# A convolution and an expert layer on one core: a shift tile of half the width, layer norm by sums on ScalarE, eleven gather slots, the last output chunk accumulated in memory, first loads in other queues, and a new written order

## The chip, the cores and the metric

The kernel runs on one core of a Trainium2 chip. The metric is the device time of one execution in microseconds (us); lower is better. Engines are named as the profile names them: PE multiplies matrices, DVE is the vector engine, ACT the scalar engine with its function tables, POOL the general engine, which here mostly issues indirect transfers, and SP issues the plain transfers. SBUF is the memory on the chip in 128 partitions, PSUM the small memory that PE writes.

## The reference

Two layers share one normalised input, and their sum is returned (L = 2048 tokens, D = 448 columns; cut to what matters):

```python
xn = _layernorm(x)                         # mean and variance over the 448 columns
# layer A: a long convolution along the tokens, one filter for each column
dt = exp(log_dt)
P  = exp((dt * A)[:, :, None] * l)         # A complex, 448 x 256; l = 0..2047
K  = einsum("dn,dnl,dn->dl", C, P, dt * B).real
yA = irfft(rfft(xn, 4096) * rfft(K, 4096))[:2048] + xn * Dskip
# layer B: one expert out of 4096 for each token and each of 16 heads
q      = einsum("nd,dhc->nhc", xn, w_q)    # two halves of 256 for each head
s1, s2 = q1 @ k1.T, q2 @ k2.T              # 64 scores each
e      = argmax(s1) * 64 + argmax(s2)
act    = gelu(einsum("nd,nhd->nh", xn, u[e]))
yB     = einsum("nh,nhd->nd", act, v[e])
return x + yA + yB
```

Only the best of each half is kept, so the softmax over the chosen experts is over one element and is 1.

## The kernel before

`Kernel.plan` registers steps, each with an engine, the steps it depends on and the buffers it takes from rings and gives back. Each step belongs to a named stream. The string `ORDER`, some 3,000 characters long, is the order in which the steps are written into the program: each character names a stream through `CODE`, and takes that stream's next step. Each engine runs its own instructions strictly in the order written. A step waits where a dependency is not met or a buffer is not free, and what stands behind it on the same engine or in the same queue waits too.

The work falls into these parts:

- **Parameters.** Six parameter arrays of 448 KB and `log_dt` are loaded on SP. DVE, ACT and POOL make from them phases and decays (the tiles `pv`, `pw`, `px`), which go to the memory tensors `tp_d` and `tt_d`. `dt` goes through memory once (`dt_d`) to spread it over the partitions; `pv<-pv,dt` on POOL (L432) needs it.
- **Combine** (`combine`, 16 heads). The query weights are multiplied with the keys in advance: 32 loads `wq` of 448 KB on SP, PE's `wc` (L862), a copy on ACT, a transpose on PE, and the result kept as `W`.
- **Layer norm** (`ln`, two of the 16 tiles of 128 tokens at a time). Tile `xx` is loaded, DVE takes the statistics (`BATCH_NORM_STATS2` L909 and `BATCH_NORM_AGGREGATE` L913) and a reciprocal square root by three iterations on 128x2 numbers, ACT writes the normalised tile (L925), SP stores it as `xn_d`.
- **Input of the convolution** (`u_step`): PE `up` (L724), ACT `vst` (L727), a store to `vu_d`.
- **Scores** (`score`): PE `sc` (L961, L970), the maximum and its index on DVE and ACT, the index list through memory (`idx_d`) to `ig`.
- **Filter tables** (`batch`, 56 of 8 columns). PE makes exponents `lg` (L579, L581), ACT the magnitudes `mg` (L590, L592). DVE makes integer phases `ph`: a first row (L610), then four doublings that add a shifted step from the tile `st` to the rows there are (L614). `st` is made by `steps` (L547) for four batches at a time; `ph` holds two batches. ACT reads `ph` and makes cosine and sine in `CS` (L629, L632, L635). DVE's products L660, L662, L664 and L666 make `zi` and `mg` out of `mg` and `CS`, and PE sums them to `kp` (L682); `kt`, `vp` and `VK` follow.
- **Convolution** (`conv`, chunks of 128, 128, 128 and 64 columns): PE `U` from `VU` and `VK` (L798, L779 for the last chunk), ACT `us`, DVE's product `cp` (L808, L786), PE's inverse transform `ip` (L830, L825), ACT `tq` (L837), a store to `t_d` (L842).
- **Experts** (`experts`, 16 tiles, four groups of four indirect gathers): POOL gathers a row of u and v for each token and head as `ue` (L1083, 448 KB each), DVE takes the dot with the token `xr` (L1091), short steps on ACT and DVE make the factors `A` (L1114), PE sums `po` (L1121), ACT copies to `ob`, POOL issues a store that adds to the output in memory (L1136).
- **Final** (`final`, for each chunk, four groups of four token tiles): `tl` is loaded from `t_d` and `hl` from a constant, PE `po` (L1178), ACT copies, POOL issues a store that adds to the output (L1192). The last chunk is done in another way: its part of the output is loaded back as `bb`, DVE adds to it (L1182) and SP writes it with a plain store; its constant comes as one tile `hb`.

Gather slots, `wq`, `xx`, `W`, `tl`, `bb`, `hb` and others come from one pool of 4 KB tiles; the number of gather slots in it is `UE`.

Of the kernel before, what the change touches and what calls it, by code (L numbers as in the profile page):

```python
# [8 lines left out]
F32 = mybir.dt.float32  # L9
# [106 lines left out]
class Plan:  # L116
# [57 lines left out]
    "44H444HH1HH2704HH7HH2HHH46HH7HH24444I6H4444H47H8CH22NI2H4241DE4HHC88142OC78D4D127H4H1EKECH74C44FLKF4CHHDL47HDEEFKDFFL24H"  # L174
    "27EC4J42HMF2HDC227KLI272223QEI47DC44E4346CDFFDK441C4QE4C9FDE978L88FDRQ9M4CREE94J74497J75RCKF5F8LQ4KCD977R71D4wE77E9778CL"
    "FFDEDAE6YFF7AYK9QHHLQANH7OQRHR9GR8S8AH9wQZH9HRaTwRHAQGHeRQYTHRQTHGQTRTRYHNHRHOSTQJTAQGMTHTeTHbQTRTTReTQUcQdQRVeNfRIVOWgg"
    "PXRQRfQPPPxBRRggHSxQTfgRxTyHeTRggIRZxTgwMXJxQKTyxHLyyfgQKLgzxQRh!!HRNRyyOz#xSPyyHQgzT!MH#QQxxggzgJTT$h!RyhTxRxR#HQRgfhgT"
    "#HQyTbghyh$yzQx!fHz!#NxyReOyiQ#TeHTHx$gyxRwYHeyxRTwxzQeUKHSeVQR!whgLhHwRjgHgcQQKQx!PRydzgY#yHRLHTbyIJRINHR#ThgThHx$bhHhH"
    "TOgKcLkRHVaTyMSdxgzxgT!!QiHxQzRyKHxQj#eHTyPTQRTyTHhxQfyTz!Hk#H%LggRRz$JhQMxH!iHjRRfhHRgxKg#TLHkyIfYhygTW#exyeTSexiX$KLYg"
    "lxKlLNMeyjzO!IHQzHgxKy!mygLPK#yTkTMxmQ#Hyl$ggwJQRHhzLRh!Thgmg!HezQfxhRex#gK#eQHwRwxThheHyxLgRgHR$y%QfggRHNxxOUiyjwfyzQ!z"  # L180
    "TMx!hy#byZSQggVVT#cQeHxyHRykHlgHHgzx$a!hRxJHgQ!gQHzTIYmhKTy&x#gLTh#digXIKTeQRyRTLJYP$fNjggTRhRlxOgeHyyHkHQzfKgh!gLxmzHHh"
# [12 lines left out]
    "gqg$xzjy!eq#yhykorgoxspcoixgh#hypqyygwxnwb$zdoggpsqf!yhwhqayp!ehjgqegrgfohgzpehss#opxqxxogk#wpfgqoexegzhg$pyotg!!qiZhqxh"
    "xgjxiojggxppzrlhh#yk#geysqytm$lnszykm!gzixf%qre!yhgjtehgf#yhs#yxgxgx&kyhfzsggxyleeggy!gzgh!i#jtyxh#zg!h!hal$mlgxzemk(g$f"
    "geyymgfyxxheyghzg#f!z!#ehegxliw#bwgxgggjhhhkwgwg$gh#)i$ymh*yehcjgdlklyehxmf&xxggf(yyeyxhmgxzy!y%igxzjz+fg!x)(e!(gZek#gz#"
    "ygglhxhh$xy!y##yxmgx*)ghywihc$gdjzgk*ha)f*ieexbg!gjywzfggfge!xheey##ghyhggh+xilzggkgxxlg!hjhh+gmzmwe!ykX$fxyxglih#eymgf#"
    "wgx+gjh$yefxhxzxye!gzxg!yZhg#ey%#ygzxkigca!l!hyxj$gdmgghhyzgxkhlh#ey#xfyehgzg!y!yxmxxfgzgifye#yx$xjz#heg!g!egzwwgkhylxhh"
    "i$gmyjgxwfxklwyyg#h#mzogh!yn!hoxigz$pxg#oeyyxgef#e%jyqxeppqzg!$qhgofgnZoo!pqhxehrgigypzgyqkggp#xy#qhhygop$sogpgsqx&xxofo"
    "qnpaqyzgpg-erfhesooyen!qjzggh!yxtpxfs#pgegq&oxw#egypgnqhwhiu$vojzghhq&!wptrnkkhgxhgqgsie!ufzyggoeh#ghefp#es$ggjvfygxhxny"  # L200
    "%gkuolhgmileqxhpwlgjyxzhtmxiqhg!!gjmggzrxglshshklkhuh#hlmmmhhyytij&x#kxixxyyjvz!$xv(kxllmymo!oqqqryysqszox(rs#y#yy)o$ysz"
    "y!zz!#!tz!*#q,q()#q#rtss($qr*+)ts$+s*t..+).//%&::-./:/*;;:+;;")


class Kernel:
    OPT = dict(UE=8, XX=4, CS=2, ZI=2, MG=4, KT=4, HL=2, SG=1, XR=4, OB=3, XT=1, ST=1)
# [21 lines left out]
    def alloc(s):  # L228
# [11 lines left out]
        s.t_d = dr.tile([64, 2, 32, D], F32, name="t_d")  # L240
# [14 lines left out]
        s.amt = c.tile([128, 2, 4], I32, name="amt")  # L255
        s.ph = c.tile([128, 16, 2, 2, M, 2], I32, name="ph")
# [18 lines left out]
    def consts(s):  # L275
# [6 lines left out]
        def sets():  # L282
            s.nc.gpsimd.memset(s.halfpi, HALF_PI)
            s.nc.gpsimd.memset(s.one, 1.0)
            s.nc.gpsimd.memset(s.dsk, 0.0)
            for h in range(2):
                for k in range(4):
                    s.nc.gpsimd.memset(s.amt[:, h, k:k + 1], k + 2 + 6 * h)
# [98 lines left out]
    def params(s, part):  # L387
# [145 lines left out]
    def steps(s, u):  # L533
# [9 lines left out]
        def sh():  # L543
            o["st"] = s.sm.tile([128, 4, 4, 2, M, 2], I32, name="st", bufs=s.o["ST"])
            for h in range(2):
                a = s.amt[:, h]
                s.nc.vector.tensor_tensor(out=view(o["st"], 2 * M * h, [[16 * M, 4], [4 * M, 4], [1, 2 * M]]),  # L547
                                          in0=view(o["tp"][:, 0, 0], 0, [[0, 4], [1, 4 * M], [0, 2]]),
                                          in1=view(a, 0, [[1, 4], [0, 8 * M]]), op=ALU.logical_shift_left)
        x = p.add("st_ld", "SP", xf(512, 256), l, deps=s.tp_done, take=("tpl",))  # L550
        o["ready"] = [p.add("st_v", "DVE", 2 * dv(512), sh, n=1, deps=[x, s.amt_done], take=("st",))]
        return o

    def batch(s, o, ro, b, VK, col):
# [48 lines left out]
        def row(k):  # L603
            def f():
                def rw(x, y):
                    return s.ph[:, x:y].rearrange("p r b h m x -> p r (b h m x)")
                b0 = b % 4
                if k < 0:
                    for h in range(2):
# [14 lines left out]
        def four(v):  # L624
            return view(v.rearrange("p r b h m x -> p (r b h m x)"), 2 * R * (b % 2), [[2, R], [4 * R, 16], [1, 2]])
# [636 lines left out]
```

## Time and profile before

| what | us |
|---|---|
| the three runs | 777.7, 782.04, 784.82 |
| median | 782.04 |
| the profiled run | 777.9 |
| its span, from first to last instruction | 776.1 |
| first instruction of PE | 16.56 |
| first product of the convolution on DVE (L808) | 399.72 |
| start of the last product of the convolution on DVE (L786) | 747.03 |

How to read it: the profiled run is 1.8 us longer than its span, and durations below are those of this one execution. Busy time is the sum of an engine's instructions; the time ahead of an instruction in which its engine did nothing is put down to what released it. A transfer appears twice: as its issue on SP or POOL, and as the time until its data have landed.

### The profile page before, as it was taken

To read this page: it belongs to the slowest core of one execution; us is meant where nothing else is said; L and a number is where in the kernel's file an instruction comes from. 1 tells how busy PE (TensorE), PEld (TensorE's weight loads), DVE (VectorE), ACT (ScalarE), POOL (GpSimd) and SP (SyncE) were. 2 spreads that over 40 slices of the span, in tenths; PEclk is the share of its full clock that TensorE was granted. 3 is DMA by queue.
4 is the path that set the end of the run, shared out by engine and by line. 5 is a ranking of instruction groups with operands and counts; after the bars stand their busy time and mean duration, and the time that the engine had idled before them with its cause. 6 is when DMAs were issued, how large, how long until landed. Compare 5 with 4: busy or idle time off the path is not lost.

```text
span 776.1 us, 19859 instructions
## 1 busy us (share of the span) xinstructions
PE 658.5 (85%) x7628; PEld 358.9 (46%) x7628; DVE 680.7 (88%) x1727; ACT 535.7 (69%) x1071; POOL 351.3 (45%) x303
## 2 busy tenths in 40 slices
PE   1999999998999998999888967788995775899982
PEld 0434343443434344434356644456763442577751
DVE  5878659998999999999999999799998999999840
ACT  1756237457677597665668899698797998789720
POOL 2011033353623435557455474555466585744620
PEclk9999999999999999999899997566996767699995
DMA  9997956767867859778999999898898997999996
GB/s 310 355 331 287 318 163 209 261 197 243 273 205 222 260 174 310 235 239 265 319 338 329 314 345 306 271 254 269 257 315 286 348 302 237 345 296 293 274 264 125
DMA packets 139975, 212.36 MB, mean 274 GB/s; under 512 B 45096, under 2 KB 121896, under 8 KB 139816
## 3 DMA queue, kind: packets, MB, share of 16 engines
q0 software_dynamic: 29120, 124.27, 50.2%
q1 hardware_dynamic: 110760, 86.81, 36.8%
q8 instruction: 60, 0.98, 0.5%
q14 instruction: 35, 0.29, 0.1%
HBM read 181.42 MB, written 33.29 MB: 277 GB/s over the span
## 4 chain that ended last, share of the span: by engine, by line
DVE 30%; PE 29%; DMA 19%; ACT 12%; issue 7%; POOL 1%; SPq 1%; DVEq 0%; ACTq 0%; POOLq 0%
PE sc L961 10%; DMA ue<-in_uv_dram,ig 7%; DVE ue L1091 7%; DVE zi L662 3%; DVE ph L614 3%; DVE mg L666 3%; DMA xr<-xn_d 3%; PE wc L862 3%; PE kp L682 2%; PE sc L970 2%; ACT CS L629 2%; PE ip L830 2%; ACT CS L632 2%; DVE cp L808 2%; PE up L724 2%
## 5 line engine op out<-in xcount | busy, mean ns | idle before, releaser
L1083 POOL DMA_INDIRECT ue<-in_uv_dram,ig x256 | 307.3, 1200 | 334.4 <-PE po L1121 87.1
L961 PE MATMUL sc<-W,xt 128*128 128x512 f32 x384 | 181.4, 612 | 4.6 <-ACT xt L946 3.8
L1091 DVE SCALAR_TENSOR_TENSOR ue<-ue,xr 128x448 f32<-128x448 f32 x256 | 155.8, 619 | 17.4 <-DMA ue<-in_uv_dram,ig 11.6
L961 PEld LDWEIGHTS sc<-W,xt 128*128 128x128 f32 x384 | 69.7, 192 | 93.8 <-issue 82.7
L1121 PE MATMUL po<-ue,A 128*32 128x448 f32 x512 | 70.1, 616 | 10.2 <-issue 3.9
L682 PE MATMUL kp<-mg 128*32 128x64 f32 x1792 | 64.1, 240 | 14.9 <-DVE mg L666 6.5
L590 ACT ACTIVATE mg<-lg 128x512 f32<-128x512 f32 x112 | 63.2, 597 | 18.7 <-PE lg L579 17.9
L629 ACT ACTIVATE CS<-ph 128x1024 f32<-128x1024 int32 x56 | 62.7, 1120 | 8.0 <-DVE ph L614 5.4
L662 DVE TENSOR_TENSOR zi<-mg,CS 128x1024 f32<-128x1024 f32 x56 | 68.2, 1218 | 0.0
L666 DVE TENSOR_TENSOR mg<-mg,CS 128x1024 f32<-128x1024 f32 x56 | 68.2, 1217 | 0.0
L614 DVE CUSTOM_DVE_ANT_0 ph<-st,ph 128x512 uint16<-128x512 uint16 (+2 forms) x84 | 65.1, 775 | 0.3
L635 ACT ACTIVATE CS<-CS,halfpi 128x1024 f32<-128x1024 f32 x56 | 64.4, 1151 | 0.5
L682 PE MATMUL kp<-zi 128*32 128x64 f32 x1792 | 63.4, 238 | 0.0
L632 ACT ACTIVATE CS<-ph 128x1024 f32<-128x1024 int32 x56 | 63.1, 1127 | 0.1
L682 PEld LDWEIGHTS kp<-mg 128*32 128x32 f32 x1792 | 46.5, 121 | 35.3 <-issue 8.6
L702 PE MATMUL vp<-f,kt 128*64 128x128 f32 x448 | 42.0, 319 | 21.9 <-DVE kt L693 9.3
L985 DVE TENSOR_REDUCE mx<-sc 128x8 f32<-128x512 f32 x64 | 43.7, 683 | 14.5 <-PE sc L970 10.8
L579 PE MATMUL lg<-lc,rt 32*128 32x512 f32 x112 | 40.4, 564 | 14.4 <-ACT mg L590 10.8
L682 PEld LDWEIGHTS kp<-zi 128*32 128x32 f32 x1792 | 48.8, 123 | 0.1
L702 PEld LDWEIGHTS vp<-f,kt 128*64 128x64 f32 x448 | 27.8, 156 | 45.3 <-DVE kt L693 9.0
L798 PE MATMUL U<-VU,g 128*64 128x128 f32 x384 | 42.2, 299 | 5.4 <-DVE cp L808 3.4
L830 PE MATMUL ip<-cp,e 64*128 64x256 f32 x384 | 45.4, 383 | 0.2 <-ACT tq L837 0.2
(246 smaller groups left out, 1221.3 us busy)
## 6 DMA issues: line engine op xcount, KB each, us to landing
wq<-in_wq_dram SPq DMA_DIRECT2D x32, 448.0 KB
xr<-xn_d SPq DMA_DIRECT2D x64, 224.0 KB
vu_d<-vst SPq DMA_DIRECT2D x64, 112.0 KB
VU<-vu_d SPq DMA_DIRECT2D x12, 512.0 KB
t_d<-tq SPq DMA_DIRECT2D x24, 256.0 KB
tl<-t_d SPq DMA_DIRECT2D x12, 512.0 KB
ue<-in_uv_dram,ig POOLq DMA_INDIRECT x256, 6.4
xx<-in_x_dram SPq DMA_DIRECT2D x16, 224.0 KB
```

The lines of the kernel that those rows point to most:

```text
L614: s.nc.vector.tensor_tensor(out=rw(n, 2 * n), in0=rw(0, n), in1=o["st"][:, k, b0:b0 + 2].rearrange("p b h m x -> p (b h m x)")[:, None].to ...
L629: s.nc.scalar.activation(CS[:, 1].rearrange("p (m r x) -> p m r x", r=16, x=2), four(s.ph), AF.Sin, scale=SC)
L632: s.nc.scalar.activation(B["CS"][:, 0].rearrange("p (m r x) -> p m r x", r=16, x=2), four(s.ph), AF.Abs)
L635: s.nc.scalar.activation(B["CS"][:, 0], B["CS"][:, 0], AF.Sin, scale=-SC, bias=s.halfpi)
L662: V.tensor_tensor(out=zi[:, 512:], in0=mg[:, 512:], in1=CS[:, 1], op=ALU.mult)
L666: V.tensor_tensor(out=mg[:, 512:], in0=mg[:, 512:], in1=CS[:, 0], op=ALU.mult)
L682: s.nc.tensor.matmul(kp[32 * c:32 * c + 32, 64 * gi:64 * gi + 64], T[ri][:, 1024 + m:1056 + m], view(T[ri], m, [[512, 2], [1, 32]]), start ...
L702: s.nc.tensor.matmul(vp[64 * ri:64 * ri + 64, 128 * gi:128 * gi + 128], B["kt"][:, 64 * gi:64 * gi + 64], s.f1[:, ri], start=True, stop=True)
L961: s.nc.tensor.matmul(B["sc", q].rearrange("p a b -> p (a b)"), B["xt"][:, i], w, start=(q % 2 == 0 and i == 0), stop=(q % 2 == 1 and i == 2))
L1083: s.nc.gpsimd.indirect_dma_start(out=ue, out_offset=None, in_=s.io["uv"], in_offset=bass.IndirectOffsetOnAxis(ap=s.IDX[t][:, c, g:g + 1].b ...
L1091: s.nc.vector.scalar_tensor_tensor(Q["ue", c][:, :D], Q["ue", c][:, :D], 1.0, B["xr", c], op0=ALU.mult, op1=ALU.mult, accum_out=Q["dot"][: ...
L1121: s.nc.tensor.matmul(B["po"][32 * c:32 * c + 32, :D], Q["A"][:, c], Q["ue", c][:, D:], start=(g == 0), stop=(g == 3))
```

## The change

1. The shift tile `st` holds [2, 8, 2M] words in place of [4, 4, 2M, 2]: two DVE shifts of 256 elements for four batches in place of two of 512. The pair of halves `x`, innermost in `ph` before, goes outward: [row, x, h, batch, m]. The first row becomes one instruction of 128 elements in place of two of 64; the doublings keep their sizes. ACT's two reads of `ph` in `trig` and `trig2` change with it: before, two neighbouring words and then a jump of 128 words, now single words with a jump of 64 words (256 bytes).
2. Layer norm: the two statistics instructions on DVE go. ACT makes the negative mean (Copy with scale -1/D and a sum) and the sum of squares (Square with that mean as bias and a sum), two passes of 448 elements for a tile, chained from tile to tile.
3. `UE` goes from 8 to 11. The scratch memory of dynamic transfers is set to 4096 bytes (16384 before, by default).
4. The last chunk of `final` takes the path of the others: `tl` and `hl`, a copy on ACT, an accumulating store on POOL (four more of them). `hb`, `bb` and DVE's addition go.
5. `wq` is loaded from POOL's queue, with a host layout of 3584 bytes in a row (1792 before). On SP the parameter loads come first, also with rows of 3584 bytes, and all four first tiles of x behind them.
6. `t_d` is a memory tensor of its own for each chunk, so that a store writes 64 rows of 4 KB (2 KB in the last chunk) in place of 512 rows of 512 bytes (256).
7. `ORDER` is another string.

```diff
 ORDER = (
-    "44H444HH1HH2704HH7HH2HHH46HH7HH24444I6H4444H47H8CH22NI2H4241DE4HHC88142OC78D4D127H4H1EKECH74C44FLKF4CHHDL47HDEEFKDFFL24H"
+    "444414144406C6CCC722774IIIIJJ272J2J42J2J2J22J2J212J22J2211II88IJ82K27I814K2CC4CJCC4J3JJJJJ7135CJ7MJ7NJ979MJD779NMNJDMN7ED"
...
-    OPT = dict(UE=8, XX=4, CS=2, ZI=2, MG=4, KT=4, HL=2, SG=1, XR=4, OB=3, XT=1, ST=1)
+    OPT = dict(UE=11, XX=4, CS=2, ZI=2, MG=4, KT=4, HL=2, SG=1, XR=4, OB=3, XT=1, ST=1)
...
-        s.t_d = dr.tile([64, 2, 32, D], F32, name="t_d")
+        s.t_d = [dr.tile([64, 2, 32, w], F32, name="t_d%d" % i) for i, (d0, w) in enumerate(s.chunks)]
...
-        s.amt = c.tile([128, 2, 4], I32, name="amt")
-        s.ph = c.tile([128, 16, 2, 2, M, 2], I32, name="ph")
+        s.amt = c.tile([128, 4, 2], I32, name="amt")
+        s.ph = c.tile([128, 16, 2, 2, 2, M], I32, name="ph")
...
-        for t in range(2):
-            s.ln_load(t, "w_ld")
         s.params(0)
-        for t in range(2, 4):
+        for t in range(4):
             s.ln_load(t, "w_ld")
...
-            o["st"] = s.sm.tile([128, 4, 4, 2, M, 2], I32, name="st", bufs=s.o["ST"])
-            for h in range(2):
-                a = s.amt[:, h]
-                s.nc.vector.tensor_tensor(out=view(o["st"], 2 * M * h, [[16 * M, 4], [4 * M, 4], [1, 2 * M]]),
-                                          in0=view(o["tp"][:, 0, 0], 0, [[0, 4], [1, 4 * M], [0, 2]]),
-                                          in1=view(a, 0, [[1, 4], [0, 8 * M]]), op=ALU.logical_shift_left)
+            o["st"] = s.sm.tile([128, 2, 8, 2 * M], I32, name="st", bufs=s.o["ST"])
+            for i in range(2):
+                s.nc.vector.tensor_tensor(out=o["st"][:, i], in0=view(o["tp"][:, 0, 0], 2 * M * i, [[0, 8], [1, 2 * M]]),
+                                          in1=view(s.amt, 0, [[1, 8], [0, 2 * M]]), op=ALU.logical_shift_left)
...
         def four(v):
-            return view(v.rearrange("p r b h m x -> p (r b h m x)"), 2 * R * (b % 2), [[2, R], [4 * R, 16], [1, 2]])
+            return view(v.rearrange("p r x h b m -> p (r x h b m)"), M * (b % 2), [[2 * M, 2], [1, M], [4 * R, 16], [2 * R, 2]])
...
-                s.nc.sync.dma_start(s.t_d[:, ri, 8 * q:8 * q + 8, d0:d0 + w],
-                                        Q["tq"][64 * ri:64 * ri + 64].rearrange("p k h d -> p (k h) d"))
+                s.nc.sync.dma_start(s.t_d[ck][:, ri, 8 * q:8 * q + 8].rearrange("p k d -> p (k d)"),
+                                        Q["tq"][64 * ri:64 * ri + 64].rearrange("p k h d -> p (k h d)"))
...
-                s.nc.sync.dma_start(B["w", sd], s.io["wq"][h, sd].rearrange("t p d -> p t d"))
-            x.append(p.add("w_ld", "SP", xf(256, 1792), l, take=("ue",)))
+                s.nc.gpsimd.dma_start(B["w", sd], s.io["wq"][h, sd])
+            x.append(p.add("w_lg", "POOLQ", xf(256, 1792), l, deps=[s.pl["A_re"]] if h == 0 else [], take=("ue",)))
...
-                s.nc.vector.bn_stats(B["bs"][:, i], s.XN[t][:, 0])
+                s.nc.scalar.activation(s.XN[t][:, 1], s.XN[t][:, 0], AF.Copy, scale=-1.0 / D, accum_out=B["m"][:, i:i + 1])
             return f
+
+        def sq(i, t):
+            return lambda: s.nc.scalar.activation(s.XN[t][:, 1], s.XN[t][:, 0], AF.Square, bias=B["m"][:, i:i + 1], accum_out=B["s"][:, i:i + 1])
...
-                if last:
-                    s.nc.vector.tensor_tensor(out=H["b"][:, 4 * g:4 * g + 4], in0=B["po"], in1=H["b"][:, 4 * g:4 * g + 4], op=ALU.add)
-                else:
-                    B["ob"] = B["tl"].rearrange("p x d -> p (x d)")[:, :4 * w].rearrange("p (t d) -> p t d", t=4)
-                    s.nc.scalar.activation(B["ob"], B["po"], AF.Copy)
+                B["ob"] = B["tl"].rearrange("p x d -> p (x d)")[:, :4 * w].rearrange("p (t d) -> p t d", t=4)
+                s.nc.scalar.activation(B["ob"], B["po"], AF.Copy)
...
-    nc = bacc.Bacc("TRN2", target_bir_lowering=False, num_devices=1)
+    nc = bacc.Bacc("TRN2", target_bir_lowering=False, num_devices=1, dynamic_dma_scratch_size=4096)
```

The order is seen best in the instructions of each engine. At the start of PE's program before, the weights are combined ahead of anything on x (`wc` is the combine, `xtp` and `wt` are transposes, `up` the convolution's input):

```order
L862 MATMUL wc<-wq,kk 64x448 x4
L943 MATMUL xtp<-ident,xx 128x128 x4
L943 MATMUL xtp<-ident,xx 64x128
L875 MATMUL wt__220<-ident,wt__218 128x128 x3
L875 MATMUL wt__220<-ident,wt__218 64x128
L862 MATMUL wc<-wq,kk 64x448 x8
```

The same place on PE after the change:

```order
L716 MATMUL up<-xx,f_92 128x448 x2
L854 MATMUL wc<-wq,kk 64x448 x4
L716 MATMUL up<-xx,f_92 128x448
L854 MATMUL wc<-wq,kk 64x448 x4
L716 MATMUL up<-xx,f_92 128x448
L854 MATMUL wc<-wq,kk 64x448 x4
```

PE's first instruction needed `wq` and the keys; now it needs a normalised tile of x, and the first four tiles come ahead of the third combine.

On POOL, the part from the parameter products to the first gathers, before:

```order
L432 TENSOR_TENSOR pw<-pv 128x896
L432 TENSOR_TENSOR pw<-pv,pw 128x896
L432 TENSOR_TENSOR pv<-pv,dt 128x896
L494 TENSOR_TENSOR pw<-pw 128x896
L1083 DMA ue<-in_uv_dram,ig 128x896 x42
```

After:

```order
L430 TENSOR_TENSOR pw<-pv 128x896
L847 DMA wq<-in_wq_dram 128x896
L430 TENSOR_TENSOR pw<-pv,pw 128x896
L847 DMA wq<-in_wq_dram 128x896 x13
L430 TENSOR_TENSOR pv<-pv,dt 128x896
L847 DMA wq<-in_wq_dram 128x896 x14
L492 TENSOR_TENSOR pw<-pw 128x896
L847 DMA wq<-in_wq_dram 128x896 x4
L1075 DMA ue<-in_uv_dram,ig 128x896 x33
```

The 32 loads of `wq` now stand between POOL's four products, 14 of them ahead of the one that needs `dt`; the load of `dt` on SP, which stood behind 21 of them, has none ahead of it.

The end of DVE's program before (`cp` is the convolution's product, `A` the experts' factors, `bb` the last chunk of the output):

```order
L1114 TENSOR_TENSOR A<-mask,th 128x128
L786 TENSOR_TENSOR cp<-us_8749,U 128x512 x2
L1107 SCALAR_TENSOR_TENSOR th<-th,dw 128x4
L786 TENSOR_TENSOR cp<-us_8749,U 128x512
L1114 TENSOR_TENSOR A<-mask,th 128x128
L786 TENSOR_TENSOR cp<-us_8749,U 128x512
L1182 TENSOR_TENSOR bb<-po_9063,bb 128x256
```

After:

```order
L778 TENSOR_TENSOR cp<-us_8630,U 128x512
L1083 SCALAR_TENSOR_TENSOR ue,dot<-ue,xr 128x448
L1102 TENSOR_TENSOR dw<-dot,ig 128x4
L1099 SCALAR_TENSOR_TENSOR th<-th,dw 128x4
L1093 SCALAR_TENSOR_TENSOR x_8908<-x_8908,dot 128x4
L1106 TENSOR_TENSOR A<-mask,th 128x128
L1083 SCALAR_TENSOR_TENSOR ue,dot<-ue,xr 128x448 x4
```

The last product of the convolution has moved ahead of the last two expert groups, whose last `A` is now DVE's last instruction. On POOL four accumulating stores `out_dram<-tl 128x4x64` stand at the very end.

Counted up to DVE's first `cp`, before and after: products of the filter tables 19 and 18 sets, dots 109 and 105, shifts for `st` 12 and 10, first rows of `ph` 20 and 10, doublings 40 and 38. All of layer norm lies ahead of it in both. 74 of ACT's 112 reads of `ph` come after it in the changed order.

More of the change, by code (lines that the diff above doesn't have):

```diff
@@ L178 @@
[L178 to L181, printed above, removed]
@@ L287, in sets @@
                 for k in range(4):
-                    s.nc.gpsimd.memset(s.amt[:, h, k:k + 1], k + 2 + 6 * h)
+                    s.nc.gpsimd.memset(s.amt[:, k, h:h + 1], k + 2 + 6 * h)
         x0 = s.amt_done = p.add("c_g", "POOL", 1600, sets)
@@ L1196, in final @@
[L1196 to L1203 removed]
+                s.nc.gpsimd.dma_start(o, B["ob"], accum_op=ALU.add)
```

138 lines of the change are left out of this document (55 added, 83 removed).

## The prediction

> **What bounds the kernel now.** I read the page's head first, then busy time by stretch, then the timeline at the joints between the stretches, then DVE's waits and the chain of waits at the end. The head gives the span and each engine's busy share:
>
> ```profile
> span 776.1 us, 19859 instructions
> PE 658.5 (85%) x7628; PEld 358.9 (46%) x7628; DVE 680.7 (88%) x1727; ACT 535.7 (69%) x1071; POOL 351.3 (45%) x303
> ```
>
> The program around the span adds 1.8 us (the profiled run took 777.9). DVE and PE are near each other, so the average does not say which one decides. The table of stretches does (columns: stretch, length, busy time of each engine, granted TensorE clock, DMA share, GB/s):
>
> ```profile
> 0.00:16.60 16.60, 0.04 (x1) 0.07 (x2) 8.31 (x16) 1.28 (x1) 5.75 (x17) 1.00 0.90 298
> 16.60:126.00 109.40, 104.57 (x379) 43.47 (x380) 83.04 (x163) 59.07 (x144) 15.87 (x12) 1.00 0.84 287
> 126.00:399.70 273.70, 256.89 (x2101) 111.56 (x2099) 261.57 (x724) 180.10 (x386) 130.55 (x110) 0.99 0.78 249
> 399.70:700.00 300.30, 241.20 (x3930) 161.45 (x3932) 282.71 (x719) 257.50 (x464) 173.22 (x145) 0.81 0.96 298
> 700.00:747.70 47.70, 45.20 (x1009) 34.96 (x1004) 43.38 (x109) 34.55 (x73) 21.21 (x17) 1.00 0.99 288
> 747.70:776.10 28.40, 10.56 (x224) 7.40 (x216) 1.71 (x5) 3.17 (x8) 4.73 (x4) 0.64 0.87 154
> ```
>
> From 16.6 to 126 us PE is the full engine (104.6 of 109.4). From 126 on DVE is as full (261.6 of 273.7 beside PE's 256.9), and from 399.7 to 747.7 DVE has 326.1 of 348.0 us against PE's 286.4, so there it is the bound. The last 28.4 us are a chain of transfers. I cut at 399.7 because DVE issues the first product of the convolution there, and PE had been ready earlier:
>
> ```profile
> 16.56 3.67 PE L862 MATMUL wc<-wq,kk 128*64 128x448 f32 x7 [16.56 <-DMA wq<-in_wq_dram]
> 387.16 0.44 PE L798 MATMUL U<-VU,g 128*64 128x128 f32 x4 [0.59 <-DVE eq L992]
> 399.72 0.68 DVE L808 TENSOR_TENSOR cp<-us,U 128x512 f32<-128x512 f32 x1
> ```
>
> PE starts that convolution at 387.2 and DVE reaches it 12.5 us later, with other work queued ahead on DVE. So up to the cut DVE is late by 12.5 us, and no saving on DVE is worth more than that before PE's own path decides.
>
> **The change, first part (0 to the first product).** The durations (busy us, mean ns of one, idle before):
>
> ```profile
> L909 DVE BATCH_NORM_STATS2 bst<-xx 128x6 f32<-128x448 f32 x16 | 9.7, 619 | 3.8 <-DMA xx<-in_x_dram 3.8
> L913 DVE BATCH_NORM_AGGREGATE mv<-bst 128x2 f32<-128x6 f32 x16 | 2.6, 172 | 0.0
> L547 DVE TENSOR_TENSOR st<-tpl,amt 128x512 int32<-128x512 int32 x28 | 18.0, 683 | 0.0
> L610 DVE TENSOR_SCALAR ph<-tpl 128x64 int32<-128x64 int32 x56 | 8.6, 205 | 1.0 <-ACT CS L632 1.0
> L662 DVE TENSOR_TENSOR zi<-mg,CS 128x1024 f32<-128x1024 f32 x56 | 68.2, 1218 | 0.0
> L660 DVE SCALAR_TENSOR_TENSOR zi<-mg,CS 128x512 f32<-128x512 f32 x56 | 38.3, 685 | 1.8 <-ACT CS L629 1.6
> L1091 DVE SCALAR_TENSOR_TENSOR ue<-ue,xr 128x448 f32<-128x448 f32 x256 | 155.8, 619 | 17.4 <-DMA ue<-in_uv_dram,ig 11.6
> ```
>
> Layer norm's 9.7 + 2.6 = 12.3 us leave DVE. All of it lies in this part. Halving a step from 1024 to 512 elements saves 1218 - 685 = 533 ns, so 256 elements are estimated at 683 - 267 = 0.42 us. The new order puts 10 shifts here in place of 12: 12 x 0.683 - 10 x 0.42 = 4.0 us. The first phase row is 10 instructions of an estimated 0.28 us (205 ns for 64 elements plus 64 more at the same slope) in place of 20 of 0.205: 1.3 us. One set of four products (2 x 1.218 + 2 x 0.685 = 3.8 us) and 4 dots (4 x 0.70 with their accumulator read, 2.8 us) now stand behind the first product. DVE's 352.9 us become 328.7, 24 less.
>
> Layer norm adds 32 passes of 448 elements to ACT:
>
> ```profile
> L727 ACT ACTIVATE vst<-up 128x448 f32<-128x448 f32 x32 | 17.5, 547 | 15.6 <-PE up L724 14.9 <-issue 0.6
> L925 ACT ACTIVATE xx<-xx,q,y 128x448 f32<-128x448 f32 x16 | 11.9, 756 | 14.6 <-DVE q L921 14.6
> pw<-in_C_im_dram SPq DMA_DIRECT2D x1, 448.0 KB
> ```
>
> At 0.55 to 0.76 us, I take 0.70 for a pass with a sum, they cost 22 us. ACT is idle for 399.7 - 240.5 = 159 us here, which hides them, except at the start: x now stands behind six parameter loads of 448 KB, like the one in the last row, and lc, about 3.3 MB with the first tile, so that tile lands near 11.3 us at the 298 GB/s of the first stretch, where it was used at 3.8. Six passes of the first three tiles, three parameter passes (896 elements, 0.92 us estimated from L727 and a slope of 0.82 ns worked out below), a seventh pass and the normalisation come before PE has anything, since its first instruction is now the step on x and not the combine: 7 x 0.70 + 2.8 + 0.8, some 8.5 us, and DVE's short chain between them. That is about 20.5 us against 16.56: PE is 4 us late (bounds 0 and 7). In exchange PE's idle time between 16.6 and 387 shrinks. It is 370.6 less about 351.4 busy, 19 us, partly for DVE's sake; I take 5 back. PE's first convolution matmul then stands at 386 and DVE's product at about 388, so **term 1 is -12 us**, since DVE's own 24 are capped by PE. Bounds: -20 (PE's idle time nearly gone) and -3 (PE 7 late and nothing recovered beyond DVE's lag).
>
> The wq loads on POOL: an issue of a plain transfer there takes about 1.03 us (store row below), 32 take 33 us. POOL waits in that time anyway:
>
> ```profile
> POOL ue L1083 <- DMA ig<-idx_d: 40.7, 1, 40.7
> POOL pv L432 <- DMA dt<-dt_d: 32.1, 1, 32.1
> ```
>
> Fourteen of them stand ahead of the tensor product that waited 32.1 us for dt, and 18 behind it and so behind that wait. dt's load no longer stands behind wq loads on SP, so this wait should shrink. I cost it at nothing; were dt as late as before, the later combines would starve, which is inside term 1's -3 end.
>
> **Second part (first to last product).** DVE gets the 6.6 us moved and two phase doublings (1.3), and loses 16 x 0.683 - 18 x 0.42 = 3.4 us of shifts and 36 x 0.205 - 18 x 0.28 = 2.4 us of first rows: 326.1 becomes 328. It idles for 21.9 us, of which these waits are for transfers:
>
> ```profile
> DVE ue L1091 <- DMA ue<-in_uv_dram,ig: 7.2, 8, 2.4
> DVE ue L1091 <- DMA xr<-xn_d: 3.8, 2, 3.6
> DVE cp L786 <- DMA t_d<-tq: 1.2, 1, 1.2
> ```
>
> Eleven slots let gathers run three further ahead, and t_d's rows grow from 512 bytes to 4 KB. I let half of the 12.2 us go. 328 + 16 = 344 against 348.0: **term 2 is -4 us**, bounds -15 (the waits all go, and half of the rest) and +5 (nothing goes, new order a little worse).
>
> ACT's reads of ph are the unknown. Before, each read took two neighbouring words, then jumped; now each word is 256 bytes from the last one. The nearest rows:
>
> ```profile
> L629 ACT ACTIVATE CS<-ph 128x1024 f32<-128x1024 int32 x56 | 62.7, 1120 | 8.0 <-DVE ph L614 5.4
> L590 ACT ACTIVATE mg<-lg 128x512 f32<-128x512 f32 x112 | 63.2, 597 | 18.7 <-PE lg L579 17.9
> L803 ACT ACTIVATE us<-U 128x256 f32<-128x256 f32 x48 | 18.1, 386 | 1.6 <-PE U L798 1.3 <-DVE cp L808 0.4
> L706 ACT ACTIVATE VK<-vp 128x256 f32<-128x256 f32 x56 | 21.1, 380 | 1.8 <-PE vp L702 1.7
> ```
>
> L706 reads one word in every 128 bytes, though from PSUM, and takes 380 ns where the plain L803 takes 386. That bounds the cost below at about nothing (-0.1 us a read). Above, I allow a second access for each word: (597 - 386)/256 = 0.82 ns, times 1024, +0.84 us. I take nothing, by L706. [...]
>
> **The tail.** Last come a DVE product at 747.03 and a chain through memory:
>
> ```profile
> 753.06 8.74 DMA t_d<-tq
> 763.17 6.13 DMA tl<-t_d
> 456.49 4.22 DMA t_d<-tq
> L1182 DVE TENSOR_TENSOR bb<-po,bb 128x256 f32<-128x256 f32 x4 | 1.7, 425 | 23.2 <-PE po L1178 23.2
> L1136 POOL DMA_DIRECT2D out_dram<-ob x16 | 16.4, 1028 | 0.2 <-ACT mg L590 0.2
> L1192 POOL DMA_DIRECT2D out_dram<-tl x12 | 17.0, 1416 | 22.0 <-ACT tl L1185 12.9 <-DMA out_dram<-ob 7.6 <-DVE ue L1091 1.4
> out_dram<-ob POOLq DMA_DIRECT2D x16, 224.0 KB, 6.2
> out_dram<-tl POOLq DMA_DIRECT2D x12, 256.0 KB, 7.2
> ```
>
> DVE's last row becomes an expert mask, with the last product some 6 us ahead of it. Behind that mask: PE 1, ACT 0.5, POOL's store 1.2 to issue and 6.2 to land (the next store of the same columns waits for it), that store 1.3, four more of the last chunk 5.2, and 7.2 to land: 22.6 us. The path by t_d, with its store at 4.2 in place of 8.74 (the price of the wide rows earlier), is some 2 us shorter. Against 28.4 I take **-5 us**, bounds -9 (128 KB land sooner) and +3 (the four added stores wait for the one before them, and land late).
>
> **The sum.** -12 - 4 - 5 = -21 on the profiled 777.9: 756.9. The median shown is 782.04, 4.1 above that run; I go half of it up: **759 us**.
>
> **The rivals.** Chances in brackets. One row of the page is wanted here, the GB/s of each fortieth of the span:
>
> ```profile
> GB/s 310 355 331 287 318 163 209 261 197 243 273 205 222 260 174 310 235 239 265 319 338 329 314 345 306 271 254 269 257 315 286 348 302 237 345 296 293 274 264 125
> ```
>
>  The forecast [0.48], by its own bounds 750 to 771.
>
> *ACT takes over, slower* [0.18]. A read of ph costs +0.84 us. 74 of the 112 lie behind the first product: +62 us on ACT's 292 of 348, which makes 354. At the 0.94 that DVE reaches today the part takes about 377 in place of 344: +33, **793 us**. It decides from about +0.43 us a read (ACT 324, as full as DVE). For it: nothing in SBUF shows such a pattern at full rate; DVE already waits for CS at L660. Against: L706.
>
> *No gain* [0.20]. The bytes decide: the DMA share is 0.96 and 0.99 in the second part, so slots add queued gathers and no data, and waits stay; PE is 7 late at the start and recovers nothing; the added stores lengthen the tail by 3. -3, 0, +3 and the 2 above it: about **779 us**. For it: the DMA share. Against: that share is time in flight, at 298 GB/s on average where slices reach 355.
>
> *Large gain* [0.14]. PE's 19 us of idle were DVE's doing, so term 1 is the whole 24; the waits for transfers vanish in the second part, -12; tail -5: about **738 us**. For it: DVE's fullness. Against: PE's first 110 us are full as they are.
>
> **How the numbers follow.** The range, 740 to 793, leaves out half of the large gain and half of the slower case, 0.16. Within 1% of 782.04 (774 to 790) is about what a measurement can tell from no change. Faster: 0.48 + 0.14 + a little of the no-gain case = 0.63. Same: the rest of that and a little of the slower case under its full price = 0.19. Slower: 0.18.
>
> **What would show it.** Right: stats gone from DVE; PE's first instruction near 20 us; first product near 388; DVE's L547 near 0.42 us; ACT's reads of ph at 1.12; t_d's stores near 4 us at the end; the tail near 23. Wrong: reads of ph at 1.5 us or more with DVE waiting for CS; PE starting behind 24 or starving for wq; the gather waits as long as before; the four last stores one after another's landing.

## The result and the profile after

The changed kernel took 854.26 us (median of 4 runs, 850.26 to 857.18) against 783.43 us for the kernel before (4 runs): 1.091 times as long, 95% interval 1.082 to 1.099. The forecast was 759 us. Executions over 1.5% above the fastest of their kernel (beside `a_pairs` 5 of 13 of the kernel before, 781.5 to 787.6 us against 769.5) are left out of the ratios and intervals, so that a ratio can differ from the quotient of two medians. The profiled run took 850.26 us. The head of its page, and its busy time by stretch (length, PE, PEld, DVE, ACT, POOL, granted clock, DMA share, GB/s), cut at PE's first work, at the first product of the convolution on DVE, behind the last one, and where the last stores begin:

```profile
span 848.5 us, 19848 instructions
## 1 busy us (share of the span) xinstructions
PE 669.0 (79%) x7628; PEld 367.2 (43%) x7628; DVE 666.6 (79%) x1663; ACT 651.8 (77%) x1139; POOL 365.9 (43%) x339
```

```profile
0.00:20.00 20.00, 0.05 (x1) 0.06 (x1) 12.59 (x35) 9.19 (x20) 10.90 (x28) 1.00 0.92 325
20.00:126.00 106.00, 99.93 (x365) 40.14 (x366) 73.24 (x131) 57.55 (x151) 27.12 (x33) 1.00 0.77 271
126.00:400.60 274.60, 256.46 (x2013) 112.02 (x2015) 245.51 (x671) 215.38 (x408) 128.59 (x111) 0.99 0.76 251
400.60:813.60 413.00, 297.23 (x4990) 206.50 (x4981) 330.93 (x812) 364.12 (x545) 188.02 (x159) 0.81 0.82 248
813.60:818.00 4.40, 4.40 (x86) 3.29 (x84) 3.36 (x15) 1.64 (x7) 1.34 (x1) 1.00 0.93 144
818.00:848.50 30.50, 10.97 (x200) 5.23 (x192) 0.97 (x6) 3.91 (x12) 9.97 (x8) 0.65 0.85 142
```

DVE did become lighter (666.6 us against 680.7), but in the long second part it is no longer the fullest engine: ACT has 364 of 413 us, where it had 292 of 348. The groups that changed (busy us, mean ns, idle before):

```profile
L621 ACT ACTIVATE CS<-ph 128x1024 f32<-128x1024 int32 x56 | 112.4, 2007 | 4.6 <-DVE ph L607 4.6
L624 ACT ACTIVATE CS<-ph 128x1024 f32<-128x1024 int32 x56 | 112.5, 2008 | 0.0
L627 ACT ACTIVATE CS<-CS,halfpi 128x1024 f32<-128x1024 f32 x56 | 64.6, 1153 | 0.7
L544 DVE TENSOR_TENSOR st<-tpl,amt 128x256 int32<-128x256 int32 x28 | 10.5, 417 | 0.0
L604 DVE TENSOR_SCALAR ph<-tpl 128x128 int32<-128x128 int32 x28 | 6.7, 240 | 21.9 <-ACT CS L624 21.7
L899 ACT ACTIVATE xx<-xx 128x448 f32<-128x448 f32 x16 | 9.3, 583 | 10.0 <-DMA xx<-in_x_dram 10.0
L903 ACT ACTIVATE xx<-xx,m 128x448 f32<-128x448 f32 x16 | 10.7, 668 | 0.3
```

The shift takes 0.417 us as estimated, and 7.5 us are saved there. ACT's two reads of `ph` take 2.007 us in place of 1.12: 0.885 us more, 112 times, 99 us. DVE's first phase row now waits 21.7 us until ACT has read the tile it must overwrite. DVE's waits in the second part are nearly all for ACT, 74.8 us in sum, where before 6.0 were for ACT and 12.2 for transfers. The longest of them now (us in total, times, longest):

```profile
DVE kt L685 <- ACT kt L682: 15.7, 14, 2.8
DVE ph L604 <- ACT CS L624: 14.5, 8, 3.4
DVE x L1093 <- ACT x L1090: 10.8, 9, 2.4
DVE th L1099 <- ACT th L1096: 10.0, 10, 2.3
DVE mg L656 <- ACT CS L627: 9.0, 7, 2.6
```

### The profile page after: what moved, and what is told of

It is laid out like the page before. It is cut to its first block, busy times and chain, and to the rows that moved or that the text cites. A ratio compares the mean times of both kernels' runs of the same rounds, so it can differ in the third digit from the quotient of the medians.

```text
span 848.5 us, 19848 instructions
## 1 busy us (share of the span) xinstructions
PE 669.0 (79%) x7628; PEld 367.2 (43%) x7628; DVE 666.6 (79%) x1663; ACT 651.8 (77%) x1139; POOL 365.9 (43%) x339
## 4 chain that ended last, share of the span: by engine, by line
ACT 42%; PE 24%; DVE 16%; issue 8%; DMA 7%; POOL 2%; SPq 1%; POOLq 0%; ACTq 0%; DVEq 0%
ACT CS L624 11%; ACT CS L621 10%; PE sc L953 8%; ACT CS L627 4%; ACT L631 3%; DVE ue L1083 2%; DMA ue<-in_uv_dram,ig 2%; PE ip L822 2%; PE U L790 2%; DVE ph L607 2%; PE kp L674 2%; ACT L586 2%; PE po L1113 2%; ACT mg L588 2%; PE lg L575 2%
## 5 line engine op out<-in xcount | busy, mean ns | idle before, releaser
L1075 POOL DMA_INDIRECT ue<-in_uv_dram,ig x256 | 300.5, 1174 | 394.8 <-PE po L1113 121.1
L1083 DVE SCALAR_TENSOR_TENSOR ue<-ue,xr 128x448 f32<-128x448 f32 x256 | 152.7, 617 | 7.8 <-DMA ue<-in_uv_dram,ig 3.8
L621 ACT ACTIVATE CS<-ph 128x1024 f32<-128x1024 int32 x56 | 112.4, 2007 | 4.6 <-DVE ph L607 4.6
L624 ACT ACTIVATE CS<-ph 128x1024 f32<-128x1024 int32 x56 | 112.5, 2008 | 0.0
L575 PE MATMUL lg<-lc,rt 32*128 32x512 f32 x112 | 46.0, 571 | 66.0 <-ACT mg L586 44.8
L607 DVE CUSTOM_DVE_ANT_0 ph<-st,ph 128x256 uint16<-128x256 uint16 (+1 forms) x112 | 72.9, 651 | 0.2
L627 ACT ACTIVATE CS<-CS,halfpi 128x1024 f32<-128x1024 f32 x56 | 64.6, 1153 | 0.7
L674 PEld LDWEIGHTS kp<-mg 128*32 128x32 f32 x1792 | 46.8, 123 | 39.9 <-issue 12.2
L575 PEld LDWEIGHTS lg<-lc,rt 32*128 32x128 f32 x112 | 17.9, 207 | 98.3 <-ACT mg L586 52.7
L716 PE MATMUL up<-xx,f 128*128 128x448 f32 x64 | 34.3, 620 | 28.5 <-ACT xx L917 19.9
L822 PE MATMUL ip<-cp,e 64*128 64x256 f32 x384 | 49.2, 411 | 0.3 <-DVE cp L800 0.3
```

The lines of the kernel that those rows point to most:

```text
L575: s.nc.tensor.matmul(ps, ro["rt"][rs, i], s.lc[rs, :512], start=True, stop=True)
L607: s.nc.vector.tensor_tensor(out=ph[:, n:2 * n], in0=ph[:, :n], in1=o["st"][:, b0 // 2, 2 * k:2 * k + 2].rearrange("p h n -> p (h n)")[:, N ...
L621: s.nc.scalar.activation(CS[:, 1].rearrange("p (h m r x) -> p h m r x", h=2, r=16, x=2), four(s.ph), AF.Sin, scale=SC)
L624: s.nc.scalar.activation(B["CS"][:, 0].rearrange("p (h m r x) -> p h m r x", h=2, r=16, x=2), four(s.ph), AF.Abs)
L627: s.nc.scalar.activation(B["CS"][:, 0], B["CS"][:, 0], AF.Sin, scale=-SC, bias=s.halfpi)
L674: s.nc.tensor.matmul(kp[32 * c:32 * c + 32, 64 * gi:64 * gi + 64], T[ri][:, 1024 + m:1056 + m], view(T[ri], m, [[512, 2], [1, 32]]), start ...
```

## The experiments

Ratios are to the kernel before, run beside it on the same chip.

**Undo the first part, and do it alone.** `a_pairs` is the changed kernel with the tiles `st`, `amt` and `ph` of before; `b_words` is the kernel before with those of the changed one. The line that reads `ph`, as `a_pairs` has it (the shifts and first rows are left out here):

```diff
...
-            return view(v.rearrange("p r x h b m -> p (r x h b m)"), M * (b % 2), [[2 * M, 2], [1, M], [4 * R, 16], [2 * R, 2]])
+            return view(v.rearrange("p r b h m x -> p (r b h m x)"), 2 * R * (b % 2), [[2, R], [4 * R, 16], [1, 2]])
...
```

> The changed kernel with its first part undone: the wide shift tile and the old layout of ph, in which ACT reads two neighbouring words at a time. Theory (the reads of ph, 0.89 us dearer each, made ACT the bound): the two reads go back to 1.12 us each, ACT's busy time falls by 99 us to about 553, and the time goes to about 760 (750 to 775), ahead of the kernel before. Rival (the new written order with its waits is slow by itself, the reads matter little): ACT's reads fall too, but the time stays above 800. A third way (the reads are the loss and the rest of the change is worth nothing): 775 to 790.

> The kernel before with the first part of the change alone: shift tile at half width, ph read word by word. Theory: reads at 2.0 us, ACT's 292 us between the first and the last product become about 355, and the time goes to 815 to 850 though DVE does 9 us less. Rival: within 10 us of the kernel before.

Measured: `a_pairs` 774.99 us, ratio 0.999 (0.994 to 1.004); `b_words` 845.61 us, ratio 1.089 (1.078 to 1.099). The first part alone costs all that the whole change costs. The reads are 1.115 us in the one and 2.013 in the other. `a_pairs` also shows that the rest of the change gains nothing that can be measured. By the prediction's own terms it was worth about 15 us: the 21 less the 5.8 us of shifts and first rows that it took from the second part. The median lies on the border between the first and the third way of its expectation; the ratio of 0.999 speaks for the third.

**What the price hangs on.** Three kernels keep the changed layout and read it otherwise. `c_dense` reads 16 neighbouring words at a time and scatters what it writes; `d_every2` and `k_every4` read every second and every fourth word of the tile; their phases are those of other columns, so that they show the time of such a read and do not compute the layer's result.

```diff
-  four: M * (b % 2), [[2 * M, 2], [1, M], [4 * R, 16], [2 * R, 2]]
+  c_dense:  M * (b % 2), [[2 * R, 32], [2 * M, 2], [1, M]]     written to CS at [[1, 32], [32 * M, 2], [32, M]]
+  d_every2: 0, [[2, 1024]]
+  k_every4: 0, [[1, 2], [4, 512]]
```

> The changed kernel with the two reads of ph done in another sequence: sixteen neighbouring words at a time are read, and CS is written one word in every 128 bytes, to the same places. If the price is one of reads far apart and ACT's writes are free of it: 1.12 us a read, and the time is that of the run with the pairs or some 5 less (740 to 770). If a write far from the last one costs as much: 2.0 us as before and about 854.

> The changed kernel with the two reads of ph taken from every second word (8 bytes apart) of the whole tile in place of one word in 256 bytes: the phases are those of other columns, the number of words is the same. If what counts is two hits on 16 bytes, a read takes 1.12 us, and the time falls to about 760. If every word that does not adjoin the last one costs a second access, it takes 2.0 us and the time stays near 854.

> The changed kernel with the two reads of ph taken from every fourth word (16 bytes apart; the phases are those of other columns). If the price is one of each new 16 bytes: 2.0 us a read and about 850, as with words 256 bytes apart. If the price needs far jumps: 1.15 us and about 768, as with every second word.

The rows of the first read, of `c_dense`, `d_every2` and `k_every4`, one fence each:

```profile
L621 ACT ACTIVATE CS<-ph 128x1024 f32<-128x1024 int32 x56 | 112.5, 2010 | 4.6 <-DVE ph L607 4.5
```

```profile
L621 ACT ACTIVATE CS<-ph 128x1024 f32<-128x1024 int32 x56 | 64.7, 1156 | 4.6 <-DVE ph L607 4.3 <-DVE mg L658 0.2
```

```profile
L621 ACT ACTIVATE CS<-ph 128x1024 f32<-128x1024 int32 x56 | 116.6, 2081 | 4.4 <-DVE ph L607 4.4
```

Words 8 bytes apart cost next to nothing (1.156 us against 1.12 for the pairs and 1.15 for the dense L627). Words 16 bytes apart cost the full price (2.081 us), about as much as words 256 bytes apart (2.007). So the price sets in above 8 and at the latest at 16 bytes; 12 was not run. That it hangs on two hits on the same 16 bytes, as the expectation of `d_every2` supposes, is not shown: a limit elsewhere between 8 and 16 bytes would fit these runs too. The price is 0.885 us for 1024 words 256 bytes apart (0.86 ns a word). `c_dense` adds that a write of one word in 128 bytes costs the same, with reads of 16 neighbours: the second outcome of its expectation. The times: `c_dense` 846.97 us, ratio 1.091 (1.081 to 1.100); `d_every2` 767.79 us in one run, against a median of 779.25. `k_every4` took 916.62 us in one run, against 827.16, on a chip of which more below; its read time is what counts here.

**Half the price.** `h_half` reads word by word in `trig` and every second word in `trig2`.

```diff
-  trig2: four(s.ph)
+  trig2: view(ph, 0, [[2, 1024]])
```

> The changed kernel with one of the two reads of ph word by word (2.0 us) and the other from every second word (1.15 us; its phases are those of other columns). ACT between the first and the last product then has about 300 + 38 x 0.85 = 332 us. If ACT costs little until it is as full as DVE: 772 to 790. If every added microsecond on ACT costs its share, because DVE and PE wait for its results one by one: half way between 768 and 850, about 809.

Measured: 803.25 us in one run, near the 809 of its second theory; its span is 801.5 us. The heads of `d_every2` and `h_half`:

```profile
span 766.0 us, 19848 instructions
## 1 busy us (share of the span) xinstructions
PE 643.5 (84%) x7628; PEld 352.4 (46%) x7628; DVE 660.8 (86%) x1663; ACT 557.8 (73%) x1139; POOL 375.3 (49%) x339
```

```profile
span 801.5 us, 19848 instructions
## 1 busy us (share of the span) xinstructions
PE 649.4 (81%) x7628; PEld 355.5 (44%) x7628; DVE 664.2 (83%) x1663; ACT 604.3 (75%) x1139; POOL 375.5 (47%) x339
```

46.5 us more on ACT make the span 35.5 us longer; the full price, 94.0 us more (651.8), makes it 82.5 longer. That is 0.76 and 0.88 us for each. These are single executions, on more than one chip; `b_words`, run four times, is 69 us longer than the kernel before by its ratio, for 96.5 us more on ACT (632.2 against 535.7), which is 0.71. Smaller amounts than 46.5 us were not run, so whether a little more work on ACT would be free stays open.

The way it comes through shows in DVE's waits for ACT between the first and the last product: 15.2 us in `d_every2`, 40.5 in `h_half`, 74.8 in the changed kernel. The stretch grows by about as much, from 351.3 to 376.7 to 412.3 us. They are many short waits for single results of ACT, none over 3.4 us in the changed kernel.

**Where the rest of the change went.** The stretches of the kernel without the price (`d_every2`), cut as above:

```profile
0.00:20.40 20.40, 0.00 (x0) 0.00 (x0) 12.51 (x35) 9.13 (x20) 10.36 (x27) 1.00 0.89 317
20.40:126.00 105.60, 100.06 (x364) 40.13 (x364) 71.51 (x124) 56.11 (x149) 26.72 (x33) 1.00 0.76 268
126.00:379.10 253.10, 249.83 (x1984) 109.44 (x1984) 245.92 (x675) 187.31 (x409) 126.63 (x111) 1.00 0.82 271
379.10:731.10 352.00, 278.83 (x5024) 194.57 (x5014) 326.54 (x812) 299.74 (x546) 200.27 (x160) 0.86 0.93 294
731.10:766.00 34.90, 14.75 (x280) 8.21 (x276) 4.34 (x22) 5.55 (x17) 11.31 (x9) 0.74 0.85 142
```

| start of the first product, of the last, end (us) | first | last | end |
|---|---|---|---|
| before | 399.7 | 747.0 | 776.1 |
| changed, without the price (`d_every2`) | 379.1 | 730.4 | 766.0 |
| changed, with pairs (`a_pairs`) | 381.5 | 741.3 | 776.6 |
| changed | 400.6 | 812.9 | 848.5 |

The first part gains 18 to 21 us, the second gives back 4 to 12, and the tail grows from 29 to 35 or 36. Each row is one execution, and 13 executions of the kernel before, beside `a_pairs`, lay between 769.5 and 787.6 us. In the tail of `d_every2` DVE's `x` waits 10 us for ACT, where the short step stands behind a copy that waits for PE, which waits 6 us for `hl` (timeline of ACT: start, duration, and the idle time before it):

```profile
736.27 0.20 ACT L1096 ACTIVATE th<-x 128x4 f32<-128x4 f32 x1
744.59 0.60 ACT L1155 ACTIVATE tl<-po 128x512 f32<-128x512 f32 x1 [8.12 <-PE po L1151]
745.08 0.20 ACT L1090 ACTIVATE x<-dot 128x4 f32<-128x4 f32 x1
```

`e_hl` is `a_pairs` with more buffers for `hl`; `i_tail` has in addition the last eighty steps in another order, run three times (`i_tail`, `o_tail`, `r_tail`).

```diff
-                B["h"] = s.flat("hl", "hl", 256).rearrange("p (x e) -> p x e", e=32)
+                B["h"] = s.flat("q" if ck > 1 else "hl", "hl", 256).rearrange("p (x e) -> p x e", e=32)
```

> The run with the pairs, and the constant hl of the last two output chunks in tiles of the large pool in place of a ring of two buffers. Theory (the tail is 6 us longer than before since each hl load waits until PE has used the second last one, with t_d stores and tl loads queued behind it on SP and an expert step on ACT behind the copy that waits for it): PE's waits for hl (9.7 us after 728) mostly go, the stretch from the last product to the end falls from 35 to about 28 us, and the time to about 768 against 775. Rival (the four added stores that land one after another set the end): the waits for hl go, the time stays within 3 us of 775.

> The run with hl in the large pool, and its last eighty steps in another order: the short expert steps on ACT and PE and the stores to t_d ahead of three copies of the third output chunk, and that chunk's store, which waits for the last expert store to land, behind three of the last chunk's. Theory (the tail is long because the last expert group stands behind those copies and the last stores behind that landing): the wait of 4 to 9 us of DVE's x on ACT goes, the stretch from the last product to the end falls from 35 to 28 to 30 us, and the time to about 770 against 777. Rival (memory traffic sets the tail): no change.

> The same kernel as the run with the other order of the last eighty steps, for the same reason. Theory (ACT's copies and the last landing hold up the end): the stretch from the last product to the end 28 to 30 us, ratio to the kernel before 0.985 to 0.99. Rival: 0.994 as with hl in the large pool alone.

> The other order of the last eighty steps once more. Without gaps on PE: 0.985 to 0.99 if the tail's order was the loss, 0.994 if not. With gaps: 1.04 to 1.05.

`e_hl`: 777.39 us, ratio 0.994 (0.991 to 0.998), no better than `a_pairs` within the intervals. The stretch from the last product to the end did fall, from 35.3 to 29.4 us, near the theory's 28, though PE's waits for `hl` after 728 fell only from 9.7 to 6.2 us and DVE's wait for `x` from 8.8 to 4.3. But the last product itself came 6 us later (747.3 against 741.3): DVE now stood for 5.6 us ahead of a product of the last chunk, for nothing that the trace shows. The time is the rival's, by a wait that it did not name.

`i_tail`, `o_tail` and `r_tail` took 861.28, 869.04 and 869.90 us. Their stretch from the last product to the end is 30.4, 28.1 and 28.0 us, hardly shorter than the 29.4 of `e_hl`, so that the other order has no clear part in it. And a new wait came ahead of it, a product that waits until a store has landed:

```profile
DVE cp L756 <- DMA out_dram<-tl: 10.1, 1, 10.1
```

The ratios are 1.042, 1.047 and 1.042, all on chips with the gaps on PE told of next, and on those `a_pairs` was not run. So whether the tail's order is worth anything stays open.

**Parts of the change on the kernel before, in its order.** `f_slots`: eleven slots and the smaller scratch. `g_td`: `t_d` by chunks. `m_parts2`: both. `j_lnslots`, `l_parts3` and `p_parts3`, one kernel: both, and layer norm's sums on ACT. `n_xr` and `q_xr`: `t_d` by chunks, the smaller scratch, ten slots, six buffers for `xr` in place of four.

```diff
-    OPT = dict(UE=8, XX=4, CS=2, ZI=2, MG=4, KT=4, HL=2, SG=1, XR=4, OB=3, XT=1, ST=1)
+    f_slots, m_parts2, l_parts3: UE=11        n_xr: UE=10, XR=6
```

> The kernel before with eleven gather slots and the smaller scratch alone, order as before. Theory of the forecast (half of DVE's waits for transfers are for lack of slots): 4 to 8 us faster than before. Rival (the transfers themselves set when gathers land, or the written order does): within 3 us.

> The kernel before with one memory tensor for each chunk of t_d alone, order as before. Theory: the last store lands in about 4 us in place of 8.7 and the chain at the end is 4 to 5 us shorter, nothing else moves: 3 to 6 us faster. Rival (the store is slow for other traffic in the queues): within 2 us.

> The kernel before, in its order, with three parts of the change and no other: eleven slots, t_d by chunks, and layer norm's two sums on ACT in place of DVE's statistics. If the parts add and DVE's 12.5 us of lateness at the first product is the room for layer norm's 12.3: the first product at about 388 and the time 760 to 766. If PE or the waits for ACT's longer first steps take it back: 768 to 774, which is what the slots and t_d give alone.

> The same kernel as the run before with slots, t_d by chunks and layer norm's sums on ACT, since the chip of that call took 827 us for the kernel before where two others took 780, with PE's filter sums held up (86 us of gaps in which PE waited for nothing shown, against 9 to 13 us elsewhere). On a chip without those gaps: 760 to 766 if DVE's lateness at the first product is the room for layer norm, 768 to 774 if not.

> The kernel before with the slots and t_d by chunks alone. If the two add: ratio 0.987 to 0.991 to the kernel before (0.992 and 0.997 were measured apart). The difference to the run with layer norm's sums is what moving those is worth: 6 to 12 us if DVE's lateness is the room, 0 if not.

> As the run with two parts, but ten slots and six buffers for the token tiles xr in place of eleven and four. With eleven slots DVE's waits for gathers were gone and its waits for xr had grown to 15.4 us. If that wait only took the other's place: ratio 0.975 to 0.985. If the order on SP sets when xr comes: as the run with two parts.

> Slots, t_d by chunks and layer norm's sums on ACT once more, in the hope of a chip without the gaps on PE (80 to 120 us of them on two chips, 11 on two others). Without gaps: 0.97 to 0.98 to the kernel before if layer norm's 12.3 us are worth their size, 0.987 to 0.991 if nothing. With gaps: 1.015 to 1.03 as before.

> Ten slots, six xr buffers and t_d by chunks once more. Without gaps on PE: 0.975 to 0.985, with DVE's waits for xr gone. With gaps: 0.989.

| run | median us | before, beside it | ratio, 95% interval | gaps on PE |
|---|---|---|---|---|
| `f_slots` | 774.56 | 779.87 | 0.992 (0.988 to 0.997) | none |
| `g_td` | 777.25 | 779.87 | 0.997 (0.994 to 1.000) | none |
| `j_lnslots` | 839.91 | 827.16 | 1.015 (1.007 to 1.022) | 29.6 us |
| `l_parts3` | 846.22 | 831.37 | 1.025 (1.017 to 1.034) | 30.9 us |
| `m_parts2` | 833.41 | 831.37 | 1.002 (0.997 to 1.006) | 31.1 us |
| `n_xr` | 819.84 | 831.37 | 0.989 (0.985 to 0.994) | 27.7 us |
| `p_parts3` | 849.19 | 836.26 | 1.017 (1.013 to 1.022) | 34.6 us |
| `q_xr` | 817.64 | 836.26 | 0.982 (0.975 to 0.988) | 28.1 us |

The last column is the time in which PE stood idle ahead of the matmuls of the filter sums `kp`, waiting for nothing that the trace shows ("issue", with its count and the longest). The first two runs were on a chip where the kernel before takes 780 us, the others on chips where it takes about 830. The 80 to 130 us of gaps named in the expectations add to this PE's weight loads (PEld), which run beside the matmuls, so that much of the time counts twice. The rows of `f_slots`, where only the weight loads have one, and of `j_lnslots`:

```profile
PEld kp L682 <- issue: 11.3, 28, 2.5
```

```profile
PEld kp L682 <- issue: 55.5, 116, 1.5
PE kp L682 <- issue: 29.6, 72, 1.1
```

`f_slots`: of DVE's 12 us of waits the 7.2 for gathers are gone, and those for `xr` have grown from 3.8 to 15.4 us:

```profile
DVE ue L1091 <- DMA xr<-xn_d: 15.4, 5, 6.5
```

It is still 0.8% faster, as the theory of its expectation had it, but not by its mechanism: DVE's waits for transfers did not shrink. Where the gain comes from is not shown, and that its size came out as forecast was luck. `m_parts2`, which contains it, gains nothing on a chip with gaps, where its expectation was 0.987 to 0.991. `n_xr` gives `xr` two buffers more, and DVE's waits for `xr` are gone: it is the fastest against the kernel before of all that compute the whole result, by 1.1 and 1.8% (`q_xr`), on chips with gaps; it was not run on another. In `g_td` the store to `t_d` in the chain at the end falls from 8.74 to 2.84 us, and from the last product to the end it takes 24.8 us in place of 29.1, as its theory had it. But the last product came 3.3 us later in this execution, and the kernel gains only 2.6:

```profile
756.85 2.84 DMA t_d<-tq
759.97 5.72 DMA tl<-t_d
```

Layer norm's sums on ACT, in the old order, make the kernel slower than `m_parts2` beside it (846.22 against 833.41). The first product comes at 427.4 us in place of 414.7, as ACT's passes stand where DVE's statistics were written and DVE's reciprocal waits 8.2 us for them:

```profile
DVE v L914 <- ACT xx L908: 8.2, 2, 6.2
```

The chip has the gaps, so this says nothing certain of the others.

## Why the prediction was wrong, point by point

- **The step that fell** is the one on ACT's reads of `ph`: "I take nothing, by L706". The bounds named were -0.1 and +0.84 us a read; measured is +0.885, which is 99 us on ACT. L706 reads PSUM, and its 380 ns for one word in every 128 bytes did not carry over to SBUF. The slower rival took +0.84 us a read, close to that, and had the place; that the price is a second access for each word is not shown.
- **The rival's price** was too small too: +33 us, where the runs with and without the price differ by 82.5 in their spans. It let ACT's 159 idle us of the first part hide 38 of the reads, but the first product came 21 us later (379.1 and 400.6). And it let ACT reach DVE's fullness, 0.94; ACT came to 0.88. "It decides from about +0.43 us a read" did not hold either: `h_half` has just that as the mean of its two reads, and lost 35 us.
- **Term 1, -12 us:** +1 in the changed kernel, and -18 to -21 without the price, at the bound named. In `d_every2` PE started at 20.4 us (20.5 expected), and DVE had 330 us (328.7 expected). PE's idle time shrank from 19 to some 9 us (358.7 us from 20.4 to 379.1 against 349.9 busy) and not by 5, on the way to the large-gain rival.
- **Term 2, -4 us:** +4 us in `d_every2`, inside its bounds. DVE's work was as expected (326.5 us, 328 said), and its waits for transfers halved, as said (12.2 to 6.2 us, at most 4.7 of it for `xr`). But its waits for ACT rose from 6.0 to 15.2 us, which the term did not have.
- **The tail, -5 us:** +6.5 us in `d_every2`. From the last mask on it was 19.4 us (22.6 expected), but the mask came 16 us behind the last product and not 6: two expert groups stood behind copies that wait for `hl`. The sum itself had a hole here: its second part ends at the last product and its 22.6 us begin at the mask, and the 6 us between them are in neither. From the last product its own figures give 28.6 us, no gain against 28.4. The sum of the three terms without the price is -10 us, in one execution, where -21 was said.
- `wq` on POOL cost nothing that shows, as said: in the changed kernel PE's weight loads waited 1.3 us for it, and POOL's wait for `dt` fell from 32.1 to 9.5 us.

## What to carry to other kernels

Look at the distance between the words that an access pattern takes from SBUF on ACT. For 1024 words, a read of single words took 2.08 us at 16 bytes and 2.01 at 256, and a write 2.01 at 128; a dense pass took 1.15, a read of words 8 bytes apart 1.16, and one of pairs of neighbours with a jump behind each 1.12 (writes of pairs or at a shorter distance were not run). Where a layout is wider than it must be, look who reads it before halving it: 9 us saved on one engine cost 99 on the other here. Where every engine runs an order written out by hand, do not count idle time on an engine as room for longer instructions on it: of each us added to ACT here, at 69 to 73% busy, 0.7 to 0.9 came through to the end.

## What the runs showed of the hardware that was not expected

The kernel before took 780 us on two chips and 827 to 836 on two others. It was not profiled on the slower ones, but `j_lnslots` and `m_parts2` were. A single matmul of the filter sums takes nearly as long there (243 ns in `f_slots`, 245 in `j_lnslots`), but the 3,584 small matmuls overlap less: they keep PE busy for 98.3 us in place of 72.6. And PE stands idle ahead of them for 28 to 50 us in all on the slower chips, in gaps of some 0.4 us that nothing in the trace explains; on the others it is 3 us at most. PE is then fuller than DVE (690.5 against 680.6 us in `m_parts2`; 658.4 against 679.9 in `f_slots`). The cause is open. `f_slots` gained 0.8% on the one kind of chip, and `m_parts2`, which contains it, nothing on the other, so that a time is best compared with one taken beside it on the same chip.
